# Expert 0 cut at 384 rows in place of 512, the first weight splits moved ahead of the last routing, and the fifth block's router logits moved to VectorE

## The chip, the cores and the metric

The kernel runs on one core of one Trainium2 chip. The metric is the device time of one execution in microseconds (us).

## The reference

The input passes three stages. Windowed attention (4 sequences of 576 tokens, 8 heads of 64) gives x of 2304 tokens by 512. A dense gated layer of width 1536 gives a new x. A sparse layer of 8 experts of width 1024 takes two experts a token:

```python
x = sigmoid(x @ w_gate) * (x @ w_val) @ w_out           # dense layer, 512 -> 1536 -> 512
logits = x @ w_gate2                                    # sparse layer, 8 experts
noisy = logits + log1p(exp(x @ w_noise)) * noise
top2, weights = the two largest of a row, softmax over the two
for e in range(8):
    h = maximum(x[rows of e] @ w1[e], 0)
    out[rows of e] += weight * (h @ w2[e])
```

## The kernel before

**Numbers.** Each product of float32 matrices is done as three matmuls (`mm3`, L56 to L58): both operands are split into a high part and a rest, and high x high, high x rest and rest x high are summed in PSUM. A split takes one ScalarE copy (high part) and one VectorE subtraction (rest). The weights of the experts are split in `split_e` (L655 to L658), the hidden activations in `h_ev` (ScalarE L712, VectorE L713), the dense activations in `glu_high` and `glu_low`.

**Dense stage.** The 2304 tokens are six blocks of 384 (b = 0 to 5). A block passes 12 chunks (f) of the dense width: gate matmuls, value matmuls, tanh on ScalarE, a multiply and the split on VectorE and ScalarE, and one chunk later the output matmuls (`glu_out`). Attention of later tokens runs inside the chunks of earlier blocks; the last block (b = 5) has none. The order of work is written out by hand (`ORDER`, with three hooks h0, h1, h2 a chunk), and every engine follows it in program order.

**Routing.** The router logits of blocks 0 to 3 are made on VectorE during the next block: `route_V` issues, for each of 16 columns and 3 tiles of 128 tokens, one multiply-and-sum of 128x512 with a weight row that a DMA copied to all partitions (`load_wb`, two columns a load, two buffers). `VS` says how many in each phase of the chunks. Blocks 4 and 5 go another way: `route_T` transposes x on TensorE and copies it out, `route_M` multiplies it with the weights `wgn` and copies the 16 logits to VectorE. Then come small steps: `route_L1`, `route_La`, `route_Lb` (noise, the two largest, weights), `route_Lc` (one-hot sum M), `route_P` (two matmuls that count the positions, with a running `base`), `route_Q` (slot numbers and records), `route_S` (six scatters from GpSimd into the table `slots`, one row a slot). For block 4 these steps stand in chunks 1 to 8 of block 5, for block 5 after the dense stage.

**Experts.** An expert has 640 slots, 5 tiles of 128. `table` loads an expert's slots, `gather` fetches the rows of x by indirect DMA from GpSimd (the result of each block lies in `xd`), `xg_T` transposes and splits them. The width of 1024 passes in 8 chunks (f) of 128: hidden matmuls `h_mm` (12 a part of the rows, 24 for a whole expert in two halves of 320), eviction `h_ev`, and the output matmuls `y_mm`, 3 for each tile of 128 rows, 512 columns wide. Expert 0 comes in two parts. Its first `EARLY` slots are filled without the last block: the line

```python
            if b == NB - 1:
                nc.vector.tensor_tensor(base[:, 0], base[:, 0], floor, op=OP.max)
```

lifts expert 0's running position to at least `EARLY` before the last block is counted. So slots 0 to 511 are gathered (`PRE_J`) during block 5 and worked on (`PRE`) while block 5 is routed; slots 512 to 639 (`POST_J`, `POST`) follow when its scatters have landed. `NA` = 7 chunks are cut in this way; chunk 7 is done whole.

**Memory.** `load_e` fetches two chunks of expert weights (r1, r2; three buffers). The pool of the experts' weights, `e0`, lies on the right side, where the dense weights were (`pw`, 120 KiB a partition); a new tile waits until what lay there is no longer read. `h1`, `l1`, `h2`, `l2` have NA + 1 = 8 buffers of 2 KiB each; `e0` takes 123 KiB a partition in all. The clearing stores of the output (26 from one tile `zero`), the loads of weights and of tables are issued by SP in program order.

## Time and profile before

| | |
|---|---|
| median of 3 runs (lowest to highest) | 1033.37 us (1031.68 to 1035.11) |
| profiled execution: time, span of its instructions | 1034.13 us, 1032.3 us |
| mean granted TensorE clock | 0.992 of full speed |
| TensorE matmul busy | 1001.0 us, 97% of the span |
| VectorE, ScalarE busy | 573.4 us (56%), 392.2 us (38%) |
| chain of work that ended last | TensorE 91%, VectorE 5% of the span |
| last dense block, first hidden matmul of expert 0 | from about 468 us; 547.50 us |

The difference of the profiled time and its span, 1.8 us, lies before the first and behind the last instruction. PE is TensorE's matmul, PEld its weight load, DVE VectorE, ACT ScalarE, POOL GpSimd, SP the engine that issues plain DMAs. A line of the timeline has the start in us, the length, the engine, the line of the kernel, the operation, what it writes and reads, its shape and its count; in brackets the idle time of the engine before it and what ended that. Matmuls overlap, so the pitch from start to start is the cost of one, not its length. In the windows the clock is the mean granted TensorE clock as a share of full speed.

### The profile page before, as it was taken

Reading aid. Unit: us, or ns where it says so; the run is one execution under the profiler, and the core shown is the slowest. Engines: PE = TensorE matmul, PEld = TensorE weight load, DVE = VectorE, ACT = ScalarE, POOL = GpSimd, SP = SyncE. Lnnn points to the kernel's source line nnn. Section 1 sums busy time; section 2 is a strip of 40 time slices with the busy share of each in tenths; the row PEclk is TensorE's granted clock in tenths of the full one; section 3 lists DMA queues with packets and bytes.
Section 4 is the critical chain, followed back from the end, with each engine's and each line's share of the span. In section 5 each row is a group of like instructions: output and inputs, shape, how many; then the busy total and the mean of one; then the engine's idle time right before and its main releaser. Section 6 shows DMA issues by size and latency. Waiting matters only on the chain.

```text
span 1032.3 us, 16703 instructions
## 1 busy us (share of the span) xinstructions
PE 1001.0 (97%) x6460; PEld 911.8 (88%) x6460; DVE 573.4 (56%) x1602; ACT 392.2 (38%) x898; POOL 152.9 (15%) x210
## 2 busy tenths in 40 slices
PE   5899999999999999999999999999999999999995
PEld 3798999999999999999997799999989999999995
DVE  8999567677668667773326434434334343434431
ACT  7999533232333333321113233333334233333321
POOL 0000000002001100302030505050311305050303
PEclk9999999999999999999999999999999999999998
DMA  9952233322333332328134527172443627172504
GB/s 362 408 230 73 65 118 108 106 80 83 108 105 100 108 112 94 84 104 256 40 83 153 132 74 194 52 176 90 100 136 87 170 82 184 42 183 84 91 2 55
DMA packets 56569, 126.79 MB, mean 123 GB/s; under 512 B 13968, under 2 KB 14112, under 8 KB 56480
## 3 DMA queue, kind: packets, MB, share of 16 engines
q1 hardware_dynamic: 46304, 104.56, 30.3%
q0 software_dynamic: 10176, 21.07, 10.4%
q8 instruction: 53, 0.87, 0.4%
q14 instruction: 36, 0.29, 0.1%
HBM read 101.11 MB, written 24.49 MB: 122 GB/s over the span
## 4 chain that ended last, share of the span: by engine, by line
PE 91%; DVE 5%; issue 1%; DMA 1%; ACT 1%; POOL 0%; POOLq 0%; DVEq 0%; ACTq 0%
PE gv L56 10%; PE gv L58 10%; PE gv L57 10%; PE hp L58 7%; PE hp L57 7%; PE hp L56 7%; PE yacc L56 7%; PE yacc L57 7%; PE yacc L58 7%; PE acc L56 5%; PE acc L58 5%; PE acc L57 5%; PE xgp L688 2%; PE Op L307 1%; PE Sp L244 1%; PE PTp L286 1%
## 5 line engine op out<-in xcount | busy, mean ns | idle before, releaser
L56 PE MATMUL gv<-xT,W 128*128 128x384 f32 (+2 forms) x584 | 201.6, 345 | 0.4 <-ACT xT L316 0.3
L57 PE MATMUL gv<-xT,W 128*128 128x384 f32 (+2 forms) x584 | 196.6, 337 | 1.3 <-DVE xT L321 1.3
L58 PE MATMUL gv<-xT,W 128*128 128x384 f32 (+2 forms) x584 | 196.7, 337 | 0.2 <-DVE W L231 0.2
L713 DVE SCALAR_TENSOR_TENSOR hl<-hp,hh 128x320 fp32r<-128x320 f32 (+2 forms) x128 | 62.9, 492 | 195.9 <-ACT hh L712 195.8
L56 PE MATMUL hp<-xgT,h 128*128 128x320 f32 (+2 forms) x512 | 162.8, 318 | 1.8 <-ACT h L655 1.8
L58 PE MATMUL hp<-xgT,l 128*128 128x320 f32 (+2 forms) x512 | 160.4, 313 | 0.3 <-DVE l L656 0.3
L57 PE MATMUL hp<-xgT,h 128*128 128x320 f32 (+2 forms) x512 | 160.0, 313 | 0.0
L712 ACT ACTIVATE hh<-hp 128x320 fp32r<-128x320 f32 (+2 forms) x128 | 56.1, 438 | 218.5 <-PE hp L58 218.5
L420 DVE CUSTOM_DVE_ANT_0 dump<-x,wb 128x512 bf16<-128x512 f32 x192 | 132.2, 689 | 3.1
L56 PE MATMUL yacc<-h,hh 128*128 128x512 f32 (+1 forms) x328 | 127.0, 387 | 0.0
L57 PE MATMUL yacc<-l,hh 128*128 128x512 f32 (+1 forms) x328 | 126.6, 386 | 0.0
L58 PE MATMUL yacc<-h,hl 128*128 128x512 f32 (+1 forms) x328 | 126.5, 386 | 0.0
L522 POOL DMA_INDIRECT slots<-rec,sli x36 | 38.7, 1075 | 517.3 <-DVE rec L512 428.8
L56 PEld LDWEIGHTS gv<-xT,W 128*128 128x128 f32 x584 | 110.3, 189 | 5.1 <-issue 1.9
L746 POOL DMA_INDIRECT out<-yo,tb x40 | 66.3, 1658 | 324.9 <-ACT yo L742 315.7
L57 PEld LDWEIGHTS gv<-xT,W 128*128 128x128 f32 x584 | 110.4, 189 | 3.1 <-DVE xT L321 1.5
L58 PEld LDWEIGHTS gv<-xT,W 128*128 128x128 f32 x584 | 110.2, 189 | 0.5 <-DVE W L231 0.5
L342 DVE SCALAR_TENSOR_TENSOR th<-th,gv 128x384 f32<-128x384 f32 x72 | 39.8, 553 | 119.8 <-PE gv L58 106.0
L56 PEld LDWEIGHTS hp<-xgT,h 128*128 128x128 f32 x512 | 96.7, 189 | 4.4 <-ACT h L655 2.2
L58 PEld LDWEIGHTS hp<-xgT,l 128*128 128x128 f32 x512 | 96.5, 189 | 2.3 <-DVE l L656 1.2
L57 PEld LDWEIGHTS hp<-xgT,h 128*128 128x128 f32 x512 | 96.7, 189 | 2.0
L56 PE MATMUL acc<-W,gH 128*128 128x512 f32 x216 | 86.2, 399 | 0.0
(138 smaller groups left out, 1524.1 us busy)
## 6 DMA issues: line engine op xcount, KB each, us to landing
raw<-in_moe_w SPq DMA_DIRECT2D x36, 512.0 KB, 10.2
wb<-in_wgn SPq DMA_DIRECT2D x32, 512.0 KB, 4.0
r<-in_w SPq DMA_DIRECT2D x32, 512.0 KB, 3.7
r<-in_moe_w SPq DMA_DIRECT2D x32, 512.0 KB, 4.6
qk<-in_qk SPq DMA_DIRECT2D x15, 640.0 KB, 5.9
v<-in_v SPq DMA_DIRECT2D x32, 256.0 KB, 4.9
out<-zero SPq DMA_DIRECT2D x26, 256.0 KB, 5.2
xd<-x SPq DMA_DIRECT2D x6, 768.0 KB, 3.5
```

The lines of the kernel that those rows point to most:

```text
L56: nc.tensor.matmul(o, lh, rh, start=start, stop=False)
L57: nc.tensor.matmul(o, lh, rl, start=False, stop=False)
L58: nc.tensor.matmul(o, ll, rh, start=False, stop=stop)
L244: nc.tensor.matmul(Sp[t][h][c, r * P:(r + 1) * P], z[rows, r, c], z[rows, r, P + i * 64:P + i * 64 + P], start=True, stop=True, skip_group ...
L286: nc.tensor.transpose(p[:, k * P:(k + 1) * P], sm[:, g * 4 + k], ident)
L342: nc.vector.scalar_tensor_tensor(g, g, 1.0, gv.pop(1)[:, :BW], op0=OP.add, op1=OP.mult)
L420: nc.vector.tensor_tensor_reduce(out=dump, in0=x2[b][:, j], in1=WB[8 * b + c // 2][:, c % 2], op0=OP.mult, op1=OP.add, scale=1.0, scalar=0 ...
L522: st = nc.gpsimd.indirect_dma_start(out=slots, out_offset=bass.IndirectOffsetOnAxis(ap=sli[:, k, j:j + 1], axis=0), in_=rec[:, j, k, :], i ...
L688: nc.tensor.transpose(p[:, c], xg[:, c], ident)
L712: nc.scalar.activation(hh[:, c], o, AF.Relu)
L713: nc.vector.scalar_tensor_tensor(hl[:, c], o, 0.0, hh[:, c].bitcast(F32), op0=OP.max, op1=OP.subtract)
L746: st = nc.gpsimd.indirect_dma_start(out=out, out_offset=bass.IndirectOffsetOnAxis(ap=tb[:, j, 0:1].bitcast(I32), axis=0), in_=yo, in_offse ...
```

## The change

- `EARLY` goes from 512 to 384: expert 0's first part has three tiles, its second two. All 8 chunks are cut (`NA` is gone, `NF2` = 8 stands in its place), so the split weights have 9 buffers and `e0` 131 KiB.
- The floor is put in before block 4 is counted, so the first part holds rows of blocks 0 to 3 only.
- Block 4's logits are made by `route_V` on VectorE in chunks 1 to 8 of block 5, six products a chunk; its weight rows are loaded into buffers of the pool `eg`. Its `route_T` and `route_M` are gone; the small steps stand in chunks 8 to 11, its scatters behind chunk 11, after the first table load and gather.
- Chunks 0 and 1 of expert 0's weights are split before the last dense chunk, with three loads in place of one; chunks 2 and 3 before block 5's logits. The work around the last routing is put in another order; the first part's hidden sums use three banks (`HP`) in place of two; the transposed x has three buffers in place of two and shares them with `zero`.
- The second part's transposes stand ahead of the last first-part output matmuls; expert 1's transposes come in the last five chunks of the second part.

```diff
...
 TR = 1024
-EARLY = 512
-NA = 7
+EARLY = 384
 R0 = NT - BW
...
                 nc.tensor.transpose(p[:, c], x2[b][:, j, c], ident)
-            xt = eg.tile([P, DM], F32, tag="x2T", name="x2T", bufs=2)
+            xt = eg.tile([P, DM], F32, tag="x2T", name="x2T", bufs=BT)
             if tag in ("S1", "acc2"):
...
 
-        def load_wb(q):
-            if q < 8 * (NB - 2):
-                w = pb.tile([P, 2, DM], F32, tag="wb", name="wb", bufs=2)
+        def load_wb(q, first=False):
+            last = q // 8 == NB - 2
+            if q < 8 * (NB - 1) and (first or not last or q % 8 > 1):
+                w = (eg if last else pb).tile([P, 2, DM], F32, tag="wb", name="wb", bufs=2)
                 c = q % 8 * 2
...
                     nc.vector.tensor_tensor_reduce(
-                        out=dump, in0=x2[b][:, j], in1=WB[8 * b + c // 2][:, c % 2], op0=OP.mult, op1=OP.add,
+                        out=dumps[b == NB - 2], in0=x2[b][:, j], in1=WB[8 * b + c // 2][:, c % 2], op0=OP.mult, op1=OP.add,
                         scale=1.0, scalar=0.0, accum_out=R[b, "lg"][:, j, c:c + 1])
...
             pos = small("s2")
-            if b == NB - 1:
+            if b == NB - 2:
                 nc.vector.tensor_tensor(base[:, 0], base[:, 0], floor, op=OP.max)
...
             s2 = r2[:, i, :]
-            h1 = ep[0].tile([P, NK, P], F32R, tag="h1", name="h1", bufs=NA + 1)
-            l1 = ep[0].tile([P, NK, P], F32R, tag="l1", name="l1", bufs=NA + 1)
-            h2 = ep[0].tile([P, 512], F32R, tag="h2", name="h2", bufs=NA + 1)
-            l2 = ep[0].tile([P, 512], F32R, tag="l2", name="l2", bufs=NA + 1)
+            h1 = ep[0].tile([P, NK, P], F32R, tag="h1", name="h1", bufs=NF2 + 1)
+            l1 = ep[0].tile([P, NK, P], F32R, tag="l1", name="l1", bufs=NF2 + 1)
+            h2 = ep[0].tile([P, 512], F32R, tag="h2", name="h2", bufs=NF2 + 1)
+            l2 = ep[0].tile([P, 512], F32R, tag="l2", name="l2", bufs=NF2 + 1)
             nc.scalar.activation(h1, s1, AF.Copy)
...
             for j in range(js.start, js.stop):
-                xg = (eg if e == 0 else ep[1]).tile([P, DM], F32, tag=f"xg{e % 2}{j % 4 if e == 0 else j}", name="xg", bufs=1)
+                xg = (eg if e == 0 else ep[1]).tile([P, DM], F32, tag=f"xg{e % 2}{j % 3 if e == 0 else j}", name="xg", bufs=1)
                 nc.gpsimd.indirect_dma_start(
...
 
-        def h_mm(e, f, cols=ALL):
+        def h_mm(e, f, cols=ALL, tags=("S0", "S1")):
             h1, l1, _, _ = sp[e * NF2 + f]
...
             for i, c in enumerate(cols):
-                o = bank(("S0", "S1")[i if len(cols) > 1 else f % 2], "hp")[:, :c.stop - c.start]
+                o = bank(tags[i if len(cols) > 1 else f % len(tags)], "hp")[:, :c.stop - c.start]
                 for k in range(NK):
...
             (False, True): {
-                (2, 1): (lambda b: route_T(b, 0),),
-                (1, 2): (lambda b: route_M(b, 0),), (2, 2): (lambda b: route_T(b, 1),),
-                (1, 3): (lambda b: route_M(b, 1),), (2, 3): (lambda b: route_T(b, 2),),
-                (1, 4): (lambda b: route_M(b, 2),), (2, 4): (route_L1,),
-                (0, 5): (route_La,), (1, 5): (route_Lb,),
-                (0, 6): (route_Lc,), (1, 7): (route_P,), (0, 8): (route_Q,),
+                (2, 8): (route_L1,), (0, 9): (route_La,), (1, 9): (route_Lb,),
+                (0, 10): (route_Lc,), (2, 10): (route_P,), (0, 11): (route_Q,),
             },
...
         )
-        VS = (4, 5, 6, 4)
+        VS = ((4, 5, 6, 4), (6, 6, 6, 6))
         c0.close()
         pb = cx.enter_context(tc.tile_pool(name="pb", bufs=1, reuse_waits="tile"))
-        dump = pb.tile([P, DM], BF16, name="dump")
+        dumps = [pb.tile([P, DM], BF16, name="dump")]
         load_wb(0)
...
                 def hook(n):
-                    if mid and 1 <= f <= 10:
-                        v = sum(VS[g % 4] for g in range(1, f))
-                        m = VS[ph]
+                    if b and 1 <= f <= 10:
+                        v = sum(VS[fin][g % 4] for g in range(1, f))
+                        m = VS[fin][ph]
                         route_V(b - 1, (range(v, v + 1), range(v + 1, v + m // 2 + 1),
...
                     eg = cg.enter_context(tc.tile_pool(name="eg", bufs=1, reuse_waits="tile"))
+                    dumps.append(eg.tile([P, DM], BF16, name="dump"))
+                    for i in range(2):
+                        load_wb(8 * b + i, True)
                     wgn = eg.tile([P, NK, 16], F32, name="wgn")
...
                     nc.sync.dma_start(wgn[:, :, 8:], a["moe2_w_noise"].rearrange("(k p) e -> p k e", p=P))
-                    zero = eg.tile([P, DM], F32, name="zero")
+                    zero = eg.tile([P, DM], F32, tag="x2T", name="zero", bufs=BT)
                     nc.gpsimd.memset(zero, 0.0)
...
                         nc.sync.dma_start(out[i * P:(i + 1) * P, :], zero)
-                    if f == 8:
-                        route_S(b - 1, range(BT))
                     if f == NF1 - 3:
...
                         gather(0, PRE_J)
+                    if f == NF1 - 1:
+                        route_S(b - 1, range(BT))
                     if f == NF1 - 2:
...
                         ep[0] = ce.enter_context(tc.tile_pool(name="e0", bufs=1, side="right", reuse_waits="tile"))
-                        load_e(0)
-                        split_e(0)
+                        for c in range(3):
+                            load_e(c)
+                        for n in range(2):
+                            split_e(n)
                 prev = (b, f)
...
         pre = range(EARLY // P)
+        HP = ("S1", "S0", "acc2")
         xg_T(0, 0, "OP")
...
         xg_T(0, 2, "S1")
-        xg_T(0, 3, "OP")
-        load_e(1)
-        load_e(2)
         for j in range(BT):
-            route_T(b, j, ("S0", "acc2", "S1")[j])
-        h_mm(0, 0, PRE)
+            route_T(b, j, ("S0", "acc2", "OP")[j])
+        h_mm(0, 0, PRE, HP)
+        split_e(2)
         h_ev(0, 0, PRE)
-        split_e(1)
+        split_e(3)
         for j in range(BT):
-            route_M(b, j, ("OP", "acc2", "acc1")[j])
+            route_M(b, j, ("acc1", "acc0", "acc2")[j])
         route_L1(b)
-        h_mm(0, 1, PRE)
+        h_mm(0, 1, PRE, HP)
         route_La(b)
...
         route_Lc(b)
+        h_mm(0, 2, PRE, HP)
         h_ev(0, 1, PRE)
-        split_e(2)
-        h_mm(0, 2, PRE)
         route_P(b)
...
         y_mm(0, 1, pre)
-        split_e(3)
-        h_mm(0, 3, PRE)
+        h_mm(0, 3, PRE, HP)
+        split_e(4)
+        h_ev(0, 3, PRE)
         route_S(b, range(BT))
...
         gather(0, POST_J)
-        h_ev(0, 3, PRE)
-        for f in range(4, NA):
+        for f in range(4, NF2):
             y_mm(0, f - 2, pre)
-            split_e(f)
-            h_mm(0, f, PRE)
+            split_e(f + 1)
+            h_mm(0, f, PRE, HP)
             h_ev(0, f, PRE)
+        y_mm(0, NF2 - 2, pre)
         for j in range(EARLY // P, CT):
-            xg_T(0, j)
-        y_mm(0, NA - 2, pre)
-        split_e(NA)
-        y_mm(0, NA - 1, pre)
+            xg_T(0, j, ("OP", "S1")[j % 2])
+        y_mm(0, NF2 - 1, pre)
         nc.vector.tensor_tensor(base[:, 0], base[:, BT], ebase, op=OP.subtract)
...
     gather(1, slice(0, CT))
-    for f in range(NA):
+    for f in range(NF2):
         h_mm(0, f, POST)
...
             y_mm(0, f - 1, range(EARLY // P, CT))
-            if f <= CT:
-                xg_T(1, f - 1)
+        if f >= NF2 - CT:
+            xg_T(1, f - NF2 + CT)
         if f == 2:
-            split_e(NA + 1)
-    y_prev = (0, NA - 1, range(EARLY // P, CT))
-    for n in range(NA, NE * NF2):
+            split_e(NF2 + 1)
+    y_prev = (0, NF2 - 1, range(EARLY // P, CT))
+    for n in range(NF2, NE * NF2):
         e, f = divmod(n, NF2)
```

## Rows read from the trace of the kernel before

**Rows 1.** The page: busy time of each engine; the chain's shares.

```profile
PE 1001.0 (97%) x6460; PEld 911.8 (88%) x6460; DVE 573.4 (56%) x1602; ACT 392.2 (38%) x898; POOL 152.9 (15%) x210
...
PE 91%; DVE 5%; issue 1%; DMA 1%; ACT 1%; POOL 0%; POOLq 0%; DVEq 0%; ACTq 0%
```

**Rows 2.** Window of the last dense block: width, engines' busy times, clock, DMA.

```profile
468.00:545.00 77.00, 77.00 (x422) 71.92 (x421) 27.17 (x103) 14.96 (x30) 16.48 (x28) 1.00 0.42 127
```

**Rows 3.** TensorE in order of time: first gate matmuls of chunks 1, 5, 6.

```profile
468.17 0.33 PE L56 MATMUL gv<-xT,W 128*128 128x384 f32 x1
...
497.66 0.34 PE L56 MATMUL gv<-xT,W 128*128 128x384 f32 x1
...
503.98 0.34 PE L56 MATMUL gv<-xT,W 128*128 128x384 f32 x1
```

**Rows 4.** VectorE in order of time: two routing products in block 4.

```profile
452.99 0.69 DVE L420 CUSTOM_DVE_ANT_0 dump<-x,wb 128x512 bf16<-128x512 f32 x1
...
453.72 0.69 DVE L420 CUSTOM_DVE_ANT_0 dump<-x,wb 128x512 bf16<-128x512 f32 x1
```

**Rows 5.** The tile of the weight rows: time from issue to landing.

```profile
DMA to landing us min/median/max: 3.6/4.0/6.4
```

**Rows 6.** TensorE, first and last of 22, 12, 23, 18 like matmuls.

```profile
529.83 0.34 PE L58 MATMUL gv<-xT,W 128*128 128x384 f32 x1
...
533.47 0.34 PE L58 MATMUL gv<-xT,W 128*128 128x384 f32 x1
...
574.33 0.39 PE L56 MATMUL hp<-xgT,h 128*128 128x512 f32 x1
...
576.83 0.39 PE L58 MATMUL hp<-xgT,l 128*128 128x512 f32 x1
...
595.04 0.28 PE L57 MATMUL hp<-xgT,h 128*128 128x128 f32 x1
...
597.50 0.28 PE L58 MATMUL hp<-xgT,l 128*128 128x128 f32 x1
...
1019.24 0.28 PE L56 MATMUL yacc<-h,hh 128*128 128x256 f32 x1
...
1021.27 0.28 PE L58 MATMUL yacc<-h,hl 128*128 128x256 f32 x1
```

**Rows 7.** TensorE at the seam, in order of time; idle time before in brackets.

```profile
547.50 0.48 PE L56 MATMUL hp<-xgT,h 128*128 128x512 f32 x1
...
560.57 0.50 PE L56 MATMUL hp<-xgT,h 128*128 128x512 f32 x1 [1.78 <-ACT h L655]
...
565.20 0.23 PE L485 MATMUL posp<-M,before 128*128 128x24 f32 x1
...
569.19 0.50 PE L58 MATMUL hp<-xgT,l 128*128 128x512 f32 x1 [0.26 <-DVE l L656]
...
589.06 0.63 PE L688 MATMUL xgp<-ident,xg 128*128 128x128 f32 x4 [0.97 <-DMA xg<-xd,tb]
```

**Rows 8.** A window at the seam: width, TensorE busy, granted clock, DMA.

```profile
562.00:565.20 3.20, 3.20 (x9) 0.52 0.00 0
```

**Rows 9.** VectorE: the last block's logits, one-hot sum, weights of its records.

```profile
553.85 0.33 DVE L401 COPY lg<-lgp 128x16 f32<-128x16 f32 x3
...
559.75 0.18 DVE L477 TENSOR_TENSOR M<-oh,oh 128x24 fp32r<-128x24 f32 x1
...
567.78 0.16 DVE L512 TENSOR_TENSOR rec<-ee,smr 128x6 f32<-128x6 f32 x1
```

**Rows 10.** The chain at the second gather: start, length, what.

```profile
585.46 3.46 DMA xg<-xd,tb
```

**Rows 11.** GpSimd: issue of the next gather.

```profile
586.79 0.98 POOL L675 DMA_INDIRECT xg<-xd,tb  x1 [0.30 <-issue]
```

**Rows 12.** ScalarE: the two copies of the first weight split.

```profile
535.93 0.63 ACT L655 ACTIVATE h<-r 128x512 fp32r<-128x512 f32 x1 [0.90 <-PE acc L58]
540.20 0.63 ACT L657 ACTIVATE h<-r 128x512 fp32r<-128x512 f32 x1 [3.63 <-DMA r<-in_moe_w]
```

## The prediction

> **What bounds the kernel now.** I read the share of the chain of waits by engine first, then the stage windows, then the order of time on TensorE, VectorE, ScalarE and GpSimd around the seam between the dense part and expert 0. TensorE carries 91% of the chain and is busy for 97% of the span [rows 1]. So an edit counts only if it takes matmul time away, or a wait of TensorE. In the last dense block TensorE is busy for all of its 77 us, VectorE for 27.2 us of them [rows 2]: there VectorE has room. The waits lie at the seam, 547 to 590 us, where expert 0's first matmuls, the last block's routing and the weight splits share VectorE and ScalarE. From 611 us on the change touches nothing, and the steady stage should keep its length.
>
> **Part 1: block 4's logits leave TensorE.** From the first gate matmul of chunk 1 to that of chunk 5, four chunks with the transposes and logit matmuls in them take 497.66 - 468.17 = 29.49 us; a chunk without them takes 503.98 - 497.66 = 6.32 us, four 25.28 [rows 3]. The excess is 4.21 us. Of it the two small position matmuls, about 0.29 us as at 565.20 [rows 7] (to the matmul after it, an estimate), stay and only move. TensorE gives up **3.9 us**.
>
> In their place VectorE takes 48 products of 128x512, six in each of chunks 1 to 8. In block 4, where such products run for block 3, one starts 0.73 us after the last [rows 4], so 35 us come on top of 27: some 62 of about 73 us. Per chunk that is 6 x 0.73 = 4.4 us, and the multiply and subtract of the gate, about 0.55 us each (an estimate: 1.1 us), so 5.5 of 6.3 us. Within a chunk one product stands ahead of the multiply, three between multiply and subtract, two behind. The subtract's result is asked for only a chunk later, so the three products delay nobody. Each pair of weight rows is loaded when the pair before the last is used up, and lands in 3.6 to 6.4 us [rows 5]; it has a chunk. The 26 clearing stores now share its queue, four a chunk, behind each load; a load that is late by less than a chunk costs nothing. Where the small operations of the routing (some 6 us in all) fall in chunks 9 to 11, VectorE has no products left. I cost all of this at nothing; if the cover is gone, see the third rival.
>
> **Part 2: the cut at 384.** A hidden matmul streams the rows of its part past one 128x128 weight tile, so the cut decides how wide it is. First to last of like matmuls give the pitch [rows 6]: 512 columns (576.83 - 574.33)/11 = 0.227 us; 384: 3.64/21 = 0.173; 256: 2.03/17 = 0.119; 320, between these, 0.146 (an estimate); 128: 2.46/22 = 0.112. From 512 to 256 the price falls with the columns, but 128 is hardly below 256. Before: seven chunks of 12 at 512 and 12 at 128, and one of 24 at 320: 84 x 0.227 + 84 x 0.112 + 24 x 0.146 = 32.0 us. After: 96 x (0.173 + 0.119) = 28.1 us. The gain is **3.9 us**. The output matmuls stay 120 at 512 columns, now 3 + 2 row tiles a chunk in place of 4 + 1.
>
> The Trainium skill ("TensorE: Matmul & The Clock Gate", section "Back-to-back issue gap") gives the isolated gap of a warm matmul as columns over 2.4 GHz and a constant 2.5 ns. By that both cuts would cost 26.1 us (an estimate from that page) and the part would be worth nothing. The row at 128 columns is about twice what that rule gives, so this trace disagrees with it at the narrow end, on which the gain rests.
>
> **Part 3: the waits at the seam.** Before, TensorE waits 1.78 us at 560.57 for the split of weight chunk 2, which stands on ScalarE behind the routing's exponential; it then does 12 matmuls in 565.20 - 560.57 = 4.63 us where 2.73 are due, because a second split operand is late and because the granted clock in 562.0 to 565.2 is 0.52 of full speed, nearly all of it at the 1.2 GHz level, right after the idle time [rows 7, 8]. With 0.26 us at 569.19 and 0.97 us at 589.06 [rows 7] that is 1.78 + 1.90 + 0.26 + 0.97 = 4.9 us. The change has splits 0 and 1 done before the last dense output, split 2 ahead of hidden chunk 0's eviction and split 3 ahead of the routing, so each stands over 2 us before its matmul; and three banks for the hidden sums, with a matmul put between routing steps, give the routing room. I take the first three waits, **3.9 us**, as gone.
>
> **What is late next** is the second gather, which depends on the last routing. Count from expert 0's first hidden matmul. Before: 547.50; logits in VectorE's hands at 553.85, one-hot sum done 559.75 + 0.18 [rows 9], but the position matmul only ends its wait in TensorE's order at 565.20, and the records are complete near 567.94, 20.4 us after the start [rows 7, 9]. First gathered tile: 585.46 + 3.46 = 588.92, that is 21.0 us after the records [rows 10]: six scatters, a table load, the gather. After: hidden chunk 0 takes 12 x 0.173 = 2.08 us, the last block's logits 24 x 0.112 = 2.7; the third transposed tile has a buffer of its own, so the logits reach VectorE at about 5.0. The one-hot sum comes 6.1 later, at 11.1. TensorE gets to the position matmuls after two more hidden chunks and one output chunk (9 x 0.227 = 2.04) at 11.0. Records 2.74 later (565.20 to 567.94), at 13.8; first tile at 13.8 + 21.0 = 34.8. TensorE has until then 8 x 2.08 + 7 x 2.04 + 2.7 + 0.3 = 33.9 us of work. So it waits some 0.9 us; the second tile is 1.33 us behind the first (585.46 to 586.79 [rows 10, 11]), of which its four transposes (0.45) cover a part: 0.9 more. The 0.97 us of before comes back as about 1.8, a net **loss of 0.8 us**. Bounds: if the routing were as late as before (20.4), the wait would be 8.4 us; if it is 2 us faster than I count, nothing.
>
> **The moved splits.** Two splits now stand on ScalarE and VectorE ahead of chunk 11's tanh and multiply, and block 4's last routing step ahead of the multiply. Before, the first half of split 0 waits for ninth-chunk weights to fall free at 535.93, and the second half for its load until 540.20 [rows 12]. The pool of expert weights grows from 123 to 131 KiB a partition and grows to the left, over memory that nothing uses any more, so the first loads now lie over weights freed a chunk earlier, and land before 536. Then four ScalarE copies of about 0.52 us end at 538, VectorE's part and the routing step near 541; the dense output needs the result at 543. Cost nothing; if the load is as late as before, the four copies and subtracts follow 540.2 and the output is some 2.2 us late. SP has three loads in place of one there; behind them only the last block's store waits, much later. On GpSimd block 4's six scatters move from chunk 8 to chunk 11, behind the first gather, and end (6 x 1.3 us) long before the last block's. The first table load no longer waits for them.
>
> **Sum.** -3.9 - 3.9 - 3.9 + 0.8 = -10.9, about **-11 us**. The profiled execution had a span of 1032.3 and took 1034.13 us; it would take 1023.1. It lies 0.8 above the median of the runs, 1033.37; for the median that is **1022.4 us**.
>
> **Rivals.**
> *The gather takes it back.* The chain from records to tiles holds 21 us that the change doesn't shorten, while TensorE's work before it shrinks. If routing is later than I count by 3 to 6.7 us, TensorE waits that much more, and after such idle time the lower clock costs up to the 1.5 us (3.2 x 0.48) that it cost here: 1026 to 1030. For it: that chain is the only long latency left. Against it: VectorE has few operations between the logits and the records. Chance 0.15.
> *The first splits block the last dense chunk* (their head start isn't one): +2.2 us and perhaps the clock's 1.5, so 1024.6 to 1026.1. Chance 0.09.
> *VectorE becomes the bound of the last block: slower.* Place: chunks 1 to 8. It begins to cost when a product takes over (6.3 - 1.1)/6 = 0.87 us in the mean, waiting for its weight rows included, and eats the whole gain at 11/8 = 1.4 us a chunk more, that is 1.1 us a product; at 1.3 the run takes 1033.4 + 8 x 1.2 = 1042. For it: loads up to 6.4 us to land, now in a queue with the clearing stores. Against it: the products' own 0.73 us, and two loads in flight. Chance 0.06.
> *The narrow matmul costs only its columns.* Then both cuts cost the same, Part 2's 3.9 us are nothing, and the time is 1026.3. Against it: the pitch at 128 columns [rows 6]. Chance 0.02. The rule of the Trainium skill weighed in Part 2 says this.
>
> **How the numbers follow.** My forecast has 0.68, and by itself the range 1019.5 (both tiles in time, 1.8, and a little less) to 1025. The rivals above it reach to 1030 and more; the remaining tails are small, so 8 in 10 is 1018.8 to 1028.5. A measurement of this kernel can tell about 0.3%, 3.1 us: faster means under 1030.3. The forecast, the second and fourth rival and most of the first are faster: 0.89. Within 0.3%: the upper end of the first, the lower of the third: 0.06. Slower: 0.05.
>
> **What would show it.** The last dense block's chunks at 6.3 us each, with products on VectorE and no idle TensorE; expert 0's hidden matmuls at 0.173 and 0.119 us; no stretch at half clock between 545 and 600; one wait of TensorE, for the gathered tiles, of 1 to 2 us. Wrong: a TensorE wait for the gate multiply in the last block, a wait above 4 us for the gathered tiles, or the tanh of chunk 11 behind a weight load.

## The result, and the profile after

| | before | after |
|---|---|---|
| median (lowest to highest), 5 runs each | 1033.37 us (1031.22 to 1035.11) | 1022.19 us (1020.73 to 1025.31) |
| profiled execution: time, span | 1034.13 us, 1032.3 us | 1020.73 us, 1018.9 us |

The medians lie 11.2 us apart, where 11 were forecast and 1022.4 us predicted. The ratio estimated from the runs is 0.9906, with a 95% interval of 0.9886 to 0.9926, that is 7.6 to 11.8 us less. So part of the close hit is luck of the executions: the same code, run again beside the experiments, gained 8.2 us (see "The changed kernel again"). The two profiled executions lie 13.4 us apart. Dividing them at matmuls that both have:

| stretch on TensorE | before | after | difference |
|---|---|---|---|
| start to chunk 1 of the last dense block | 468.17 | 466.86 | -1.31 |
| chunks 1 to 4 | 29.49 | 25.51 | -3.98 |
| chunk 5 to expert 0's first hidden matmul | 49.84 | 49.36 | -0.48 |
| from there to expert 1's second chunk | 74.64 | 67.85 | -6.79 |
| from there to the end of the span | 410.16 | 409.32 | -0.84 |

The first and the last stretch are untouched by the change: their 2.15 us are what one execution differs from another. The middle three give -11.25 us. The 0.48 us are about the transposes of expert 0's fourth tile, which now stand in the next stretch. Expert 1's second chunk begins at this matmul, before and after:

```profile
622.14 0.31 PE L56 MATMUL hp<-xgT,h 128*128 128x320 f32 x1
...
609.58 0.30 PE L55 MATMUL hp<-xgT,h 128*128 128x320 f32 x1
```

First the page of the kernel after, its busy line and its chain, beside [rows 1], and the window of its last dense block (columns as in [rows 2]).

```profile
PE 991.7 (97%) x6424; PEld 907.0 (89%) x6424; DVE 601.8 (59%) x1691; ACT 392.3 (38%) x899; POOL 154.3 (15%) x210
...
PE 87%; DVE 5%; issue 4%; DMA 1%; ACT 1%; POOL 0%; another core or an unknown queue 0%; POOLq 0%; DVEq 0%; ACTq 0%
```

```profile
461.00:538.00 77.00, 77.00 (x409) 72.04 (x408) 58.03 (x209) 16.60 (x35) 12.86 (x20) 1.00 0.66 211
```

TensorE has lost 9.3 us of busy time, VectorE gained 28. In the last block TensorE is still busy all of the time, and VectorE has gone from 27 to 58 us of 77. In the next two fences, TensorE and VectorE of that block in order of time (first gate matmuls of chunks 1, 5 and 6 as in [rows 3]; two products as in [rows 4]):

```profile
466.86 0.33 PE L55 MATMUL gv<-xT,W 128*128 128x384 f32 x1
...
492.37 0.34 PE L55 MATMUL gv<-xT,W 128*128 128x384 f32 x1
...
498.69 0.34 PE L55 MATMUL gv<-xT,W 128*128 128x384 f32 x1
```

```profile
471.35 0.56 DVE L341 SCALAR_TENSOR_TENSOR th<-th,gv 128x384 f32<-128x384 f32 x1 [2.74 <-PE gv L57]
471.82 0.68 DVE L420 CUSTOM_DVE_ANT_0 dump<-x,wb 128x512 bf16<-128x512 f32 x1
...
472.55 0.69 DVE L420 CUSTOM_DVE_ANT_0 dump<-x,wb 128x512 bf16<-128x512 f32 x1
```

Chunk 5 has the length that it had before, 6.32 us; the four chunks ahead of it now cost little more (25.51 for 25.28; two position matmuls of an earlier block stand in them, at 471.08). The multiply at 471.35 has waited 2.74 us for TensorE, not TensorE for it, and the products follow each other at 0.73 us.

The seam: TensorE in order of time, with pitches as in [rows 6] and waits as in [rows 7].

```profile
541.73 0.45 PE L55 MATMUL hp<-xgT,h 128*128 128x384 f32 x1
...
554.26 0.25 PE L485 MATMUL posp<-M,before 128*128 128x24 f32 x1 [1.23 <-DVE M L477]
...
556.63 0.33 PE L55 MATMUL hp<-xgT,h 128*128 128x384 f32 x1
...
558.57 0.33 PE L57 MATMUL hp<-xgT,l 128*128 128x384 f32 x1
...
577.57 0.60 PE L688 MATMUL xgp<-ident,xg 128*128 128x128 f32 x4
578.68 0.63 PE L688 MATMUL xgp<-ident,xg 128*128 128x128 f32 x4 [0.50 <-issue]
...
581.23 0.28 PE L55 MATMUL hp<-xgT,h 128*128 128x256 f32 x1
...
583.99 0.28 PE L57 MATMUL hp<-xgT,l 128*128 128x256 f32 x1
...
604.59 0.39 PE L55 MATMUL hp<-xgT,h 128*128 128x320 f32 x1
...
608.04 0.31 PE L57 MATMUL hp<-xgT,l 128*128 128x320 f32 x1
```

The waits for splits are gone. What is left is 1.23 us for the one-hot sum M, which was not foreseen, and 0.50 us for the second gathered tile. The clock, in the window from the first hidden matmul on, stays at full speed:

```profile
541.73:580.00 38.27, 36.54 (x197) 33.11 (x198) 21.34 (x75) 13.10 (x27) 14.15 (x20) 1.00 0.44 125
```

ScalarE around the last dense chunk, in order of time: the first two splits, then the tanh.

```profile
530.41 0.63 ACT L655 ACTIVATE h<-r 128x512 fp32r<-128x512 f32 x1 [0.91 <-PE acc L57]
...
532.00 0.61 ACT L657 ACTIVATE h<-r 128x512 fp32r<-128x512 f32 x1
532.72 0.49 ACT L336 ACTIVATE th<-gv 128x384 f32<-128x384 f32 x1
```

The four copies run back to back from 530.41 on, with no wait for a load, and the tanh has its turn at 532.72.

### The profile page after: what moved, and what is told of

The parts are those of the page before. It is cut to its first block, busy times and chain, and to the rows that moved or that the text cites. A ratio compares the mean times of both kernels' runs of the same rounds, so it can differ in the third digit from the quotient of the medians.

```text
span 1018.9 us, 16753 instructions
## 1 busy us (share of the span) xinstructions
PE 991.7 (97%) x6424; PEld 907.0 (89%) x6424; DVE 601.8 (59%) x1691; ACT 392.3 (38%) x899; POOL 154.3 (15%) x210
## 4 chain that ended last, share of the span: by engine, by line
PE 87%; DVE 5%; issue 4%; DMA 1%; ACT 1%; POOL 0%; another core or an unknown queue 0%; POOLq 0%; DVEq 0%; ACTq 0%
PE gv L55 10%; PE gv L57 10%; PE gv L56 10%; PE hp L57 6%; PE hp L55 6%; PE hp L56 6%; PE yacc L55 6%; PE yacc L56 6%; PE yacc L57 6%; PE acc L55 5%; PE acc L57 5%; PE acc L56 5%; PE xgp L688 2%; PE Op L306 1%; PE Sp L243 1%
## 5 line engine op out<-in xcount | busy, mean ns | idle before, releaser
L420 DVE CUSTOM_DVE_ANT_0 dump<-x,wb 128x512 bf16<-128x512 f32 x240 | 165.3, 689 | 4.6 <-DMA wb<-in_wgn 0.4
L55 PE MATMUL hp<-xgT,h 128*128 128x320 f32 (+2 forms) x512 | 161.1, 315 | 0.1
L57 PE MATMUL hp<-xgT,l 128*128 128x320 f32 (+2 forms) x512 | 158.2, 309 | 0.0
L56 PE MATMUL hp<-xgT,h 128*128 128x320 f32 (+2 forms) x512 | 158.1, 309 | 0.0
L348 ACT ACTIVATE gH<-th 128x384 fp32r<-128x384 f32 x72 | 37.8, 524 | 127.4 <-DVE th L341 121.6
## 6 DMA issues: line engine op xcount, KB each, us to landing
raw<-in_moe_w SPq DMA_DIRECT2D x36, 512.0 KB, 10.2
```

The costliest lines, as they stand in the source:

```text
L55: nc.tensor.matmul(o, lh, rh, start=start, stop=False)
L56: nc.tensor.matmul(o, lh, rl, start=False, stop=False)
L57: nc.tensor.matmul(o, ll, rh, start=False, stop=stop)
L348: nc.scalar.activation(gh, g, AF.Copy)
L420: nc.vector.tensor_tensor_reduce(out=dumps[b == NB - 2], in0=x2[b][:, j], in1=WB[8 * b + c // 2][:, c % 2], op0=OP.mult, op1=OP.add, scale ...
```

## The experiments

Twelve runs, in four groups; each group shared a chip with runs of the kernel before (medians 1032.09, 1031.01, 1033.14 and 1031.96 us). A ratio is to the kernel before on the same chip, its 95% interval in brackets. "Over after" compares with the 1022.19 us above, which were not taken in these groups. The median of the kernel before differs by up to 2.4 us from group to group, so a smaller difference to after shows nothing by itself, and the lengths in the traces decide. The time from expert 0's first hidden matmul to expert 1's first is called the seam below: 62.86 us in the trace of after (541.73 to 604.59).

**Part 1 undone.** The fifth block's transposes and logit matmuls are back on TensorE, its products gone from VectorE; the tile of zeros has its own buffer.

```diff
...
             (False, True): {
+                (2, 1): (lambda b: route_T(b, 0),),
+                (1, 2): (lambda b: route_M(b, 0),), (2, 2): (lambda b: route_T(b, 1),),
...
-                    if b and 1 <= f <= 10:
+                    if mid and 1 <= f <= 10:
```

> Part 1 undone alone: block 4's logits go back to TensorE in chunks 1 to 4 of the last dense block, the rest stays as changed; the tile of the clearing stores has a buffer of its own here. Theory (TensorE's own time): those four chunks grow from 25.5 us to about 29.5, so the time is 1022.2 + 3.9 = 1026, or up to 1.7 less if the shared buffer costs something at the seam. Rival (the 48 products on VectorE cost the last block about what they save, and the gain came from elsewhere): within 1 us of 1022.2, with the four chunks no longer by less than 2 us.

Measured: 1026.18 us (1024.11 to 1027.46), ratio 0.9928 (0.9902 to 0.9953). TensorE at the first gate matmuls of chunks 1 and 5:

```profile
468.38 0.33 PE L55 MATMUL gv<-xT,W 128*128 128x384 f32 x1
...
497.88 0.34 PE L55 MATMUL gv<-xT,W 128*128 128x384 f32 x1
```

Chunks 1 to 4 take 497.88 - 468.38 = 29.50 us, as before the change and 3.99 more than after's, and the time is 4.0 us over after's. Part 1 is worth its 3.9.

**The second part in two pieces of 128.** The price of a narrow matmul by itself: same work, same order, twice the hidden matmuls in the second part.

```diff
-        PRE, POST = (slice(0, EARLY),), (slice(EARLY, CAP),)
+        PRE, POST = (slice(0, EARLY),), (slice(EARLY, EARLY + P), slice(EARLY + P, CAP))
```

> The second part's hidden matmuls are cut into two of 128 columns each in place of one of 256: 24 a chunk in place of 12, same columns in sum. Theory (a matmul below 256 columns hardly gets cheaper): 24 x 0.112 - 12 x 0.119 = 1.26 us more a chunk, 8 chunks 10.1 us, so 1032.3. Rival (a matmul costs its columns): the time stays within 1 us of 1022.2.

Measured: 1032.32 us (1030.91 to 1035.57), ratio 1.0003 (0.9988 to 1.0017), 10.1 us over after; its seam is 72.0 us. TensorE of that kernel in order of time, 22 pitches of one part:

```profile
587.73 0.27 PE L56 MATMUL hp<-xgT,h 128*128 128x128 f32 x1
...
590.19 0.27 PE L57 MATMUL hp<-xgT,l 128*128 128x128 f32 x1
```

That is 0.112 us each, where after's 256 columns take (583.99 - 581.23)/23 = 0.120: 96 x (2 x 0.112 - 0.120) = 10.0 us. A matmul of 128 columns costs nearly what one of 256 does. The rival by which only columns count is out, and with it the isolated gap of the Trainium skill ("TensorE: Matmul & The Clock Gate", section "Back-to-back issue gap") as a price for such a stream: by it these two kernels would lie 0.2 us apart (an estimate, 96 x 2.5 ns). That section says itself that this gap counts too little at small widths in a stream with a weight load for each matmul, and gives about 81 ns at 128 columns; the 112 ns here are more than that too.

**The order of the splits undone.** One split ahead of the last dense chunk, the others again where they stood; cut, logits and banks as after.

```diff
...
-                        for c in range(3):
-                            load_e(c)
-                        for n in range(2):
-                            split_e(n)
+                        load_e(0)
+                        split_e(0)
...
-        h_mm(0, 2, PRE, HP)
         h_ev(0, 1, PRE)
+        split_e(2)
+        h_mm(0, 2, PRE, HP)
```

> The order of the weight splits undone alone: one load and split 0 before the last dense chunk, split 1 after the first hidden eviction, split 2 behind the routing's exponential, each later split just ahead of its own hidden chunk, as in the kernel before; the cut, block 4's logits and the banks stay as changed. Theory (the waits at the seam come from the splits standing behind the routing): TensorE waits 1.5 to 2 us again for split 2, with lower clock after it, 3 to 4 us in all, so 1025 to 1026. Rival (the three banks and the third buffer of the transposed x removed the waits): within 1 us of 1022.2 and no new wait at a hidden matmul.

Measured: 1024.32 us (1023.01 to 1026.20), ratio 0.9915 (0.9889 to 0.9940): 2.1 us over after, fewer than the 3 to 4 expected and, across groups, not clear of noise. TensorE's waits in this kernel:

```profile
554.59 0.44 PE L55 MATMUL hp<-xgT,h 128*128 128x384 f32 x1 [0.70 <-ACT h L655]
...
560.88 0.44 PE L57 MATMUL hp<-xgT,l 128*128 128x384 f32 x1 [0.88 <-DVE l L656]
```

Both waits are for splits, at hidden chunks 2 and 3, 1.58 us together where before had 1.78 + 0.26 and the half clock behind; here the clock behind them is full (a stretch at half clock, 548 to 551, stands behind the logit matmuls instead). From the first hidden matmul to expert 1's second chunk this trace takes 70.38 us, where the two traces of the changed kernel take 67.85 and 69.21, so the order is worth 1.2 to 2.5 us. The waits return, but smaller. The logits come earlier here than in before (4.7 us after the first hidden matmul, for 6.4), so ScalarE would be free of the routing sooner; that this is the reason is not shown.

**The gather held back.** 18 memsets on GpSimd ahead of the second gather.

```diff
         table(1, slice(0, CT), nc.gpsimd)
+        hold = eg.tile([P, DM], F32, tag="xg02", name="hold", bufs=1)
+        for _ in range(18):
+            nc.gpsimd.memset(hold, 0.0)
         gather(0, POST_J)
```

> 18 idle fills of 128x512 on GpSimd between the table loads and the gather of expert 0's second part, 0.53 us each, 9.6 us, of which the wait for the table (2.8 us) covers a part: the gather is 6.7 us late. Theory (the gather stands on the chain with less than 0.5 us to spare): TensorE's wait at the gathered tiles grows from 0.5 to about 7 us, and some of the time after it may run at the lower clock, so 1028.5 to 1030.5. Rival (the gather has slack, other work covers it): less than 2 us more.

Measured: 1032.41 us (1030.25 to 1033.23), ratio 0.9999 (0.9987 to 1.0010), 10.2 us over after (8.6 by the seams, 71.48 for 62.86), and more than the 6.3 to 8.3 expected. GpSimd, TensorE, and a window behind the wait (third figure from the right: granted clock):

```profile
569.77 10.48 POOL L886 MEMSET hold<- 128x512 f32 x18
580.45 1.05 POOL L675 DMA_INDIRECT xg<-xd,tb  x1 [0.19 <-issue]
```

```profile
583.88 1.11 PE L688 MATMUL xgp<-ident,xg 128*128 128x128 f32 x4 [7.45 <-DMA xg<-xd,tb]
585.39 1.08 PE L688 MATMUL xgp<-ident,xg 128*128 128x128 f32 x4 [0.40 <-DMA xg<-xd,tb]
```

```profile
584.00:593.00 9.00, 8.60 (x42) 7.41 (x43) 2.04 (x5) 1.58 (x3) 3.95 (x6) 0.67 0.55 165
```

The gather goes out at 580.45 for 573.65, 6.8 us later, and the waits grow from 0.50 to 7.85 us: this chain has no slack left. Behind the wait the clock is at 0.67 in the mean for 9 us, which costs 9 x 0.33 = 3 us more (an estimate).

**The changed kernel again.** The same code, on the chip of the runs beside it, to tell the kernel from one execution.

> The changed kernel as it is, on the same chip as the runs beside it, so that they have a neighbour. Theory: 1022 us again, within 1 us, about 0.99 of the kernel before. Its profiled execution tells whether the 1.23 us that TensorE waited for the one-hot sum at 554.26 in the first trace belongs to the kernel or to that one execution: if it belongs to the kernel, the third copy of the transposed x waits some 2.6 us again and the position matmuls wait about 1.2; if to the execution, the copy waits under 0.5 and the position matmuls do not wait, as in the two runs that share this code.

Measured: 1022.83 us (1020.81 to 1025.59), ratio 0.9918 (0.9900 to 0.9936): 8.2 us under the kernel before on this chip. The 1.23 us were the execution's. The third copy of the transposed x on ScalarE, in the first trace and in this one:

```profile
544.00 0.60 ACT L388 ACTIVATE x2T<-x2Tp 128x512 f32<-128x512 f32 x1 [2.57 <-remote]
...
544.92 0.60 ACT L388 ACTIVATE x2T<-x2Tp 128x512 f32<-128x512 f32 x1 [0.26 <-PE x2Tp L383]
```

Here it waits 0.26 us, for 2.57 in the first trace, and TensorE does not wait for the one-hot sum. Two other things take its place. The gathered tiles cost 0.69 and 0.96 us, as forecast, and behind the logit matmuls the clock falls. TensorE in order of time, then the window:

```profile
547.17 2.75 PE L398 MATMUL lgp<-wgn,x2T 128*128 128x16 f32 x24
...
550.72 0.36 PE L57 MATMUL hp<-xgT,l 128*128 128x384 f32 x1
...
551.20 0.52 PE L56 MATMUL hp<-xgT,h 128*128 128x384 f32 x1
551.52 0.52 PE L57 MATMUL hp<-xgT,l 128*128 128x384 f32 x1
```

```profile
550.85:554.10 3.25, 3.25 (x12) 2.96 (x11) 2.77 (x15) 0.00 (x0) 0.00 (x0) 0.51 0.62 188
```

No idle time stands ahead of it. The pitch goes from 0.174 to 0.32 us, and 3.25 x 0.49 = 1.6 us are lost. The three middle stretches of the table above take 25.51, 49.35 and 69.21 us in this trace, 9.9 us less than before, where the first trace had 11.25.

**The zeros in another buffer.**

```diff
-                    zero = eg.tile([P, DM], F32, tag="x2T", name="zero", bufs=BT)
+                    zero = eg.tile([P, DM], F32, tag="xg02", name="zero", bufs=1)
```

> The tile of zeros no longer shares its buffer with the third transposed x, but with a buffer of expert 0's first gathered rows that is filled later. Theory (the third copy waits for the clearing stores that read the zeros): its wait goes, the logits, the one-hot sum and the records come up to 2 us earlier, the position matmuls do not wait, and the gathered tiles come in time or nearly so: 1.2 to 1.7 us less than the changed kernel, about 1020.7. Rival (that wait was a matter of one execution, and the first gather then stands behind the clearing stores): within 0.5 us of the changed kernel, or slower if the first gather is late.

Measured: 1022.46 us (1020.08 to 1023.51), ratio 0.9913 (0.9898 to 0.9929), 0.4 us under the changed kernel beside it: no difference. Sharing that buffer costs nothing that can be measured here. Whether it has a part in the late copy is not tested: the copy is late neither in this trace (0.21 us) nor in that of the kernel beside it (0.26).

**More products in the last block.** Products issued again write the same sums; the diff is that with nine a chunk, the one with seven has (3,) in place of (0, 2, 4).

```diff
+                    for _ in range(1 + (b == NB - 2 and n % 6 in (0, 2, 4))):
-                    nc.vector.tensor_tensor_reduce(
+                        nc.vector.tensor_tensor_reduce(
```

> One of each six products in the last dense block is issued twice, with the same result: seven a chunk. Forecast: VectorE has 7 x 0.73 + 1.1 = 6.2 us to do in a chunk of 6.3, so the time is that of the changed kernel, within 1 us. Rival (VectorE is already close to being the bound, through its other small operations and semaphore times): 0.2 to 0.6 us a chunk, 2 to 5 us in all.

> Three of each six products in the last dense block are issued twice, with the same results: nine a chunk. Forecast: 9 x 0.73 + 1.1 = 7.7 us in a chunk of 6.3, so chunks 1 to 8 take 1.4 us more each, some 11 us in all, and TensorE waits in each of them for the multiply or the subtract: about 1033, the level of the kernel before. Rival (the queue in front of the multiply has slack that spreads over the chunks): half of that or less. If TensorE's idle time brings the lower clock, more than 11.

Measured: seven a chunk 1023.47 us (1021.16 to 1024.63), 0.6 over the kernel as it is beside it, with the block's chunks at 6.32 us still; nine a chunk 1030.37 us (1028.35 to 1032.43), 7.5 over it, ratio 0.9990 (0.9979 to 1.0001). The window of 20 us in the ninefold kernel, its first gate matmuls of chunks 6, 7 and 8, and two of TensorE's waits:

```profile
500.00:520.00 20.00, 18.67 (x91) 15.46 (x90) 19.38 (x55) 3.01 (x6) 0.00 (x0) 1.00 0.60 205
```

```profile
502.68 0.34 PE L55 MATMUL gv<-xT,W 128*128 128x384 f32 x1
...
509.95 0.34 PE L55 MATMUL gv<-xT,W 128*128 128x384 f32 x1
...
517.25 0.34 PE L55 MATMUL gv<-xT,W 128*128 128x384 f32 x1
```

```profile
500.94 0.50 PE L57 MATMUL acc<-W,gL 128*128 128x512 f32 x1 [0.44 <-DVE gL L352]
...
533.38 0.44 PE L55 MATMUL gv<-xT,W 128*128 128x384 f32 x1 [1.25 <-ACT th L336]
```

VectorE is full (19.38 of 20) and sets the chunk: 7.27 and 7.30 us, 0.97 over the usual for the 1.4 that I had worked out. Nine products at 0.73 us leave 0.7 us of it for the multiply and the subtract, for which I had put 1.1. Chunks 1 and 2 still take their usual time, as one would expect where a result is asked for a chunk later. From chunk 4 on TensorE waits 0.42 to 0.50 us a chunk for the subtract. Chunks 3 to 8 together take 5.2 us more than after's, and chunks 9 and 10, which have no products of their own, another 3.6: VectorE still has a backlog, the routing's exponential waits for it on ScalarE, and the tanh behind that comes late (the 1.25 us). So TensorE pays partly in a place that I had not counted, and the forecast of 11 came to 8.9 in this trace and 7.5 in the medians. By the seventh product, a tenth of a microsecond more for each of the six would have cost nothing (an estimate, 0.73/6); half as many products again cost nearly all of the 8.2 us that the change gains on this chip.

**The narrow matmuls and the clock.** Nine profiled executions (after, again, and the seven variants so far) all have the row of 24 matmuls of 16 columns behind hidden chunk 0, and five of them show the half clock right behind it (the changed kernel again, the splits undone, the zeros, seven and nine products). Four kernels change that row: spread between hidden chunk 0's matmuls, issued twice, and 128 or 64 columns wide (each weight column repeated). The core of their diffs, in this order, the last for 128 columns:

```diff
+                logit[3 * k + i]()
...
-            for k in range(NK):
+            for k in (*range(NK), *range(NK)):
...
-                nc.tensor.matmul(p[:, :16], xt[:, k * P:(k + 1) * P], wgn[:, k],
+                nc.tensor.matmul(p[:, :128], xt[:, k * P:(k + 1) * P], wgn[:, k, None, :].to_broadcast([P, 8, 16]),
```

> The last block's 24 logit matmuls of 16 columns no longer stand in a row behind hidden chunk 0 but one pair behind each of its 12 matmuls of 384 columns; the copies of the logits and the chunk's eviction follow at about the same time as before. Seen so far in the changed kernel and its variants: a stretch of about 3.3 us at half clock right behind the row of narrow matmuls, without idle time ahead of it, in five of nine profiled executions, worth about 1.65 us where it comes. Theory (the row of narrow matmuls brings it): no such stretch, and a median 0.5 to 1.7 us under that of the changed kernel's 1022.5. Rival (it comes by chance of the execution, whatever stands there): the stretch shows again in about half of the profiles, and the median stays within 0.5 us of 1022.5.

> Each of the last block's logit matmuls is issued twice, the second overwriting the first with the same sums: 48 narrow matmuls in a row. By their pitch they cost 24 x 0.112 = 2.7 us more, and both TensorE's work and the routing move by that, so the wait for the gathered tiles stays. Theory (the row of narrow matmuls brings the half clock): the stretch comes in the profile, and starts before or right at the end of the row; with the clock 0.7 to 2 us more, so 1026 to 1027.5. Rival (chance): full clock throughout as likely as not, and 1025.2 in the median.

> The last block's 24 logit matmuls stream each weight column eight times over: 128 columns in place of 16, of which the copies take the first 16, so the logits are the same. Their order and number stay, and by the transposes of float32 tiles (12 of 128 columns in 1.51 us, 0.126 us each) the row takes 2.7 to 3.0 us as before. Theory (a row of matmuls with little to stream brings the half clock behind it): no half-clock stretch behind the row, and where it took 1.65 us in some executions before, a median 0 to 1 us under the changed kernel's 1022.5 plus what the row itself costs more, up to 0.3. Rival (it comes by chance, whatever stands there): the stretch shows in about half of the profiles, this one or the next.

> The same with 64 columns in place of 16, each weight column four times over. Theory: no half-clock stretch behind the row here either, if what counts is how much the matmuls stream and half of it is enough; the row takes 2.6 to 2.8 us. Rival: as likely as not the stretch shows. If it shows here and not at 128 columns, the number streamed decides in between.

Measured: between 1026.69 us (1025.68 to 1029.87), ratio 0.9948 (0.9928 to 0.9967); twice 1028.65 us (1027.39 to 1030.90), 0.9965 (0.9949 to 0.9981); 128 columns 1021.31 us (1019.33 to 1026.33), 0.9898 (0.9876 to 0.9920); 64 columns 1020.51 us (1019.57 to 1023.27), 0.9892 (0.9871 to 0.9914). Two windows of the doubled row's kernel, behind the row and behind the gathered tiles; then the seams of 128 and of 64 columns:

```profile
549.70:553.20 3.50, 3.50 (x14) 3.50 (x14) 2.72 (x15) 0.22 (x1) 0.00 (x0) 0.54 0.67 267
584.00:588.00 4.00, 3.97 (x13) 3.33 (x14) 1.31 (x4) 0.60 (x1) 2.96 (x4) 0.57 0.72 219
```

```profile
541.68:580.00 38.32, 36.46 (x197) 33.00 (x198) 21.34 (x74) 13.29 (x27) 14.12 (x20) 1.00 0.44 125
```

```profile
542.04:580.00 37.96, 37.31 (x201) 33.95 (x202) 22.29 (x77) 13.27 (x27) 14.90 (x21) 1.00 0.51 131
```

Doubled, the row has the half clock behind it, as the theory has it, and the time is 1.2 us above the 1027.5 that it allowed; in the trace a second stretch, which was not in the sum, follows the waits for the gathered tiles (1.53 and 1.00 us). Wider rows show full clock in both traces; the row takes 2.84 and 2.79 us for 2.75. But with five in nine before, two clean traces come by chance one time in five ((4/9)^2), and the medians, 1.2 and 2.0 us under the changed kernel's 1022.5, are no proven gain: the intervals of the ratios overlap with its own. The spread-out row was to have no stretch and has one (clock 0.63 from 549.7 to 553.2); there a late copy of x held TensorE for 0.92 us just before, so it isn't the clean case either, and its median, some 4 us over, is more than its trace explains (its seam is 64.5 us). Its edit also moves hidden chunk 0's eviction behind split 3 and the copies of the logits. In every trace twelve transposes of x (1.51 us) stand ahead of hidden chunk 0 as well, and no run changed them. That the row brings the half clock stays likely and open.

## Why the prediction was right, step by step

**Part 1**: forecast -3.9, measured -3.98 between the traces and 4.0 by undoing it. The products hide as costed: 0.73 us each, the loads of weight rows from 454 us on landing in 5.4 us, one wait for them of 0.4. The rival of VectorE as the bound is not here, and its threshold was sized roughly right: seven products are free, nine are not.

**Part 2**: forecast 32.0 to 28.1, with pitches 0.173 and 0.119. After: (558.57 - 556.63)/11 = 0.176 and 0.120, so 96 x 0.296 = 28.4; the estimate for 320 columns, 0.146, is (608.04 - 604.59)/23 = 0.150, which puts before at 32.1. The gain is 3.7. This is from the pitches in the traces; no run undid the cut at 384 by itself.

**Part 3**: forecast -3.9 + 0.8. The traces give waits and lost clock of 4.91 us before and 1.23 + 0.50 = 1.73 after: -3.2, but by another make-up, so that the size fits is luck. In the second trace of the same code the loss is 0.69 + 0.96 + 1.6 = 3.25, and Part 3 gives 1.7 in place of 3.1. In the first trace the loss is a late copy of x; in most others it is the gathered tiles with 0.5 to 2.1 us and, in five of nine, 1.6 us of half clock. "No stretch at half clock between 545 and 600" holds in the first trace and not in the kernel. The step that failed in it: I had put the half clock down to the idle time ahead of it, since before shows it there [rows 7, 8]; the second trace shows it with no idle time ahead. Parts 2 and 3 make 6.9 of the 7.27 us that the third and fourth stretch of the table give; 0.4 us are not assigned.

**What is late next**: the trace with 128 columns has neither late copy nor half clock. Its records on VectorE, then the two gathered tiles on TensorE:

```profile
555.26 0.16 DVE L512 TENSOR_TENSOR rec<-ee,smr 128x6 f32<-128x6 f32 x1
...
577.11 0.66 PE L688 MATMUL xgp<-ident,xg 128*128 128x128 f32 x4 [0.90 <-DMA xg<-xd,tb]
578.72 0.63 PE L688 MATMUL xgp<-ident,xg 128*128 128x128 f32 x4 [0.96 <-DMA xg<-xd,tb]
```

The records are complete 13.7 us after the first hidden matmul (forecast 13.8) and the first tile's wait ends at 577.11 - 541.68 = 35.4 us (34.8); the waits are 0.90 and 0.96 (0.9 and 0.9). There the count was right to within 0.6 us. In the two traces of the changed kernel itself the records are complete after 15.2 and 15.3 us, behind the late copy in one and the half clock in the other. The rival in which the gather takes the gain back is real as a mechanism, as the held gather shows, but in these traces the routing was at most 1.5 us later than counted, not 3 to 6.7.

**The moved splits** cost nothing, with the copies at 530.41, loads landed and the tanh on time; the second rival is out. What their order gives is 1.2 to 2.5 us by undoing it, not the 3.9 that stood for the three waits. The rest of that term may come with the earlier logits and the third bank; no run tests either by itself.

## What to carry to other kernels

Price a matmul by the pitch of its own width in the trace: from 256 columns down to 128, cutting a tile here cost almost by the number of pieces, not by their columns. An engine with 65% of a stage idle is a place to put another's narrow work, as long as its period stays below the stage's and its results are asked for later. When waits are taken away, count the longest latency chain from its first operation: here it came to within 0.6 us where nothing disturbed it, and holding the gather back shows that it has become the seam's bound.

## What the runs showed of the hardware

The half clock does not need idle time ahead of it: in the second trace of the same code it comes at 550.85 behind 24 narrow matmuls on a busy engine, and lasts 3.25 us. Idle time in turn does not always bring it: 1.23 us in the first trace and 0.69 + 0.96 in the second did not, 1.78 in before and 1.53 + 1.00 with the doubled row did. Nor does the length of the wait alone decide it. The second gathered tile with seven products a chunk and the window behind it (third figure from the right: clock), then the same tile with Part 1 undone:

```profile
580.65 0.96 PE L689 MATMUL xgp<-ident,xg 128*128 128x128 f32 x4 [0.98 <-DMA xg<-xd,tb]
```

```profile
581.80:582.80 1.00, 1.00 (x4) 0.77 (x3) 0.53 (x1) 0.44 (x1) 0.77 (x1) 0.50 0.71 221
```

```profile
584.48 0.63 PE L688 MATMUL xgp<-ident,xg 128*128 128x128 f32 x4 [1.07 <-DMA xg<-xd,tb]
```

The first had waits of 1.11 + 0.98 us and the half clock behind them, the second 0.98 + 1.07 us and full clock from 582 to 590. The Trainium skill ("TensorE: Matmul & The Clock Gate", section "HAM oscillation — how this bites in real kernels") tells of a clock that falls in waits for data; the 7.45 us wait agrees, and the stretch behind the busy row is a case beside it.

The copies of the transposed x are released 1 to 2.5 us late in three of thirteen traces of the changed kernel and its variants (the first of after, the doubled and the spread-out row). The traces name no plausible releaser, and putting the tile of zeros elsewhere did not change the median; the cause stays open.
